# Turning masked scores on TensorE instead of the DMA crossbar for the first two of eight batches

## The chip, the core and the metric

The kernel runs on one core of a Trainium2 chip. The core has a matrix engine (TensorE, PE in the profile; its weight loads are PEld), a vector engine (VectorE, DVE), a scalar engine (ScalarE, ACT), GpSimd (POOL), a queue engine that issues DMAs (SyncE, SP), and 16 DMA engines. TensorE writes to PSUM, in banks; VectorE and ScalarE read PSUM and SBUF; DMAs move data between HBM and SBUF and inside SBUF. The metric is the device time of the core in microseconds, lower is better.

## The reference

Attention with a threshold over 8 batches, 8 heads, 576 positions and 64 dimensions a head, and a layer pair behind it on 4608 tokens, d_model 512 and d_ff 2048:

```python
scores = scale * np.matmul(q, k.transpose(0, 1, 3, 2))
thresh = np.max(scores, axis=-1, keepdims=True) - tau
scores = np.where(scores >= thresh, scores, -1000000000.0)
scores = scores - np.max(scores, axis=-1, keepdims=True)
attn = np.exp(scores)
attn = attn / (np.sum(attn, axis=-1, keepdims=True) + 1e-09)
out = np.matmul(attn, v)
...
h = x @ w_in
g = h - np.tanh(h)
return (g @ w_out).astype(np.float32)
```

Inputs and outputs are float32; x is the attention output with the heads of a token side by side.

## The kernel before, in words

**Pairs and tiles.** Two heads of a batch form a pair p; there are 32 pairs, four to a batch. A pair's queries are cut into nine tiles of 128 rows (TPP = 9): four of one head, one mixed tile with the last 64 rows of both, four of the other head. There are 288 tiles, i = 9p + j. `kind(j)` calls the tiles "A" (j = 0, 2, 5, 7), "B" (1, 3, 6, 8) and "M" (4).

**A tile's way.** `scores` (L215): TensorE multiplies qT with kT and with kS (the same with its two 64-row halves swapped) into psS, a PSUM tile of two banks of which there are two (ps_big, shared with the turns of k and q); VectorE copies it to sc and takes the row's maximum (L242). `shift` (L248): VectorE makes nb, tau minus the maximum. `kink` (L256): ScalarE applies a Prelu with an extreme slope, which leaves kept scores and makes dropped ones hugely negative; the result z is bf16 in SBUF, with an A tile and its B tile side by side in one z of 1152 columns, and the M tile in zm, padded to 640. Then SP issues a crossbar transpose by DMA, zT from z (L274), one for each A-B pair of tiles and one for M, so five a pair. `weights` (L280): ScalarE takes Exp of zT into pT, of 1152 columns for two tiles, 640 for M. `attend` (L290): TensorE multiplies pT with v (psO); `norm` divides by the row sums; `emit_x` (L338) turns the pair's output into psX and xT.

**Feeding a pair.** `load` brings k, q and v by DMA (L130 to L137), `split` (L143) makes of k or q a high and a low fp16 part (GpSimd, but for pair 0 ScalarE and VectorE), `turn` (L176) turns them by nine TensorE transposes, VectorE copies the result to kT or qT (L186), and for all pairs but the first two DMAs make kS from kT (L202, L203). The two layers' weights come in 16 pieces of 512 KB (`w_load`, L460 and L456), one every four steps, cast by GpSimd four steps later (`w_cast`, L448).

**The layers.** `layers(m, tail)` gives the steps for batch m's first layer (`hidden`: four matmuls into psH, L366, then Tanh on ScalarE and g on VectorE) and batch m-1's second (`project` into psY, L392). psY lies in the pool ps_y, one bank, with one buffer. Batch 0's first layer is handed out from pair 4's fifth tile on, one `hidden` in every second step, the first in step 41; psY is first used in the next stage, from step 77 on.

**The order.** Everything is written out by hand in the loop over steps s = -7 to 292. In step s come shift(s+6), scores(s+7), kink(s+5), the tanh of the last layer step, weights(s), layer steps, attend(s-2), and the planned steps of the next pairs: k's load stands 16 steps before the pair's first scores, its split 8, k's turn 5, v's split 4, q's turn 3. Each engine runs its queue in this order, and SP issues all DMAs but pair 0's load of q, which ScalarE's queue issues.

```python
    for t in ("k", "q", "v"):
        load(0, t)
    for t in ("k", "q"):
        split(0, t, fast=True)
        turn(0, t)
```

Of the kernel before, what the change touches and what calls it, by code (L numbers as in the profile page):

```python
# [9 lines left out]
F32 = mybir.dt.float32  # L10
BF16 = mybir.dt.bfloat16
FP16 = mybir.dt.float16
AX = mybir.AxisListType
ALU = mybir.AluOpType
ACT = mybir.ActivationFunctionType
# [3 lines left out]
def kernel(  # L19
# [11 lines left out]
    nc = tc.nc  # L31
    P = 128

    B, H, S, D = q.shape
# [11 lines left out]
    HPAIR = H // 2  # L46
# [2 lines left out]
    DF_C = d_ff // P  # L49
    TPP = 9  # L50
    NTILE = NPAIR * TPP
    W = 2 * S

    AHEAD = 7
# [9 lines left out]
    const = ctx.enter_context(tc.tile_pool(name="const", bufs=1))  # L64
    ident_f16 = const.tile([P, P], FP16, name="ident_f16")
    make_identity(nc, ident_f16)
    ident_bf = const.tile([P, P], BF16, name="ident_bf")
# [35 lines left out]
    zt_pool = pool("zt", 4)  # L103
    p_pool = pool("p", 3)
# [9 lines left out]
    ps_y = pool("ps_y", 1, space=PSUM)  # L114

    ctx.enter_context(tc.manual_schedule())


    raws = {}
# [23 lines left out]
    def split(p, t, fast=False):  # L143
        r = raws.pop((p, t))[:, 0:9, :]
        hl = hl_pool.tile([P, TPP, 2, D], FP16, name=f"{t}hl", tag=t)
        if fast:
            nc.scalar.mul(out=hl[:, :, 0, :], in_=r, mul=QKSC)
            nc.vector.scalar_tensor_tensor(  # L148
                out=hl[:, :, 1, :], in0=r, scalar=QKSC, in1=hl[:, :, 0, :],
                op0=ALU.mult, op1=ALU.subtract,  # L150
            )
        else:
            x = hl_pool.tile([P, TPP, D], F32, name="xs", tag="xs")
            nc.gpsimd.tensor_scalar(  # L154
                out=x, in0=r, scalar1=QKSC, scalar2=1.0, op0=ALU.mult, op1=ALU.mult
            )
            nc.gpsimd.tensor_copy(out=hl[:, :, 0, :], in_=x)
            nc.gpsimd.tensor_tensor(  # L158
                out=hl[:, :, 1, :], in0=x, in1=hl[:, :, 0, :], op=ALU.subtract
            )  # L160
        hls[p, t] = hl

    def split_v(p):
        r, vb = raws.pop((p, "v")), vbs[p % NV]
        nc.gpsimd.tensor_copy(
            out=vb[:, :, 0:4, 0:D],
            in_=r[:, 0:8, :].rearrange("p (h c) d -> p h c d", h=2),
        )
        nc.gpsimd.tensor_copy(out=vb[0:64, :, 4, 0:D], in_=r[0:64, 8:10, :])
        nc.gpsimd.tensor_copy(out=vb[64:P, :, 5, 0:D], in_=r[64:P, 8:10, :])  # L170
# [5 lines left out]
    def turn(p, t):  # L176
        hl = hls.pop((p, t))
        ps = ps_big.tile([P, W], FP16, name=f"ps_{t}", tag="big")
        for c in range(TPP):
            nc.tensor.matmul(  # L180
                out=ps[:, c * P : (c + 1) * P],
                lhsT=hl[:, c, :, :].rearrange("p a d -> p (a d)"),
                rhs=ident_f16, is_transpose=True, start=True, stop=True,
            )
        m = qk_pool.tile([P, W], FP16, name=f"{t}T", tag=t)
        nc.vector.tensor_copy(out=m, in_=ps)  # L186
        mats[p, t] = m
        if t == "k" and p == 0:
            ps = ps_big.tile([P, W], FP16, name="ps_ks", tag="big")
            for c in range(TPP):  # L190
                for a in range(2):
                    nc.tensor.matmul(
                        out=ps[64 * a : 64 * a + 64, c * P : (c + 1) * P],
                        lhsT=hl[:, c, 1 - a, :],
                        rhs=ident_f16, is_transpose=True, start=True, stop=True,
                    )
            sw = qk_pool.tile([P, W], FP16, name="kS", tag="ks")
            nc.vector.tensor_copy(out=sw, in_=ps)
            mats[p, "ks"] = sw
        elif t == "k":  # L200
            sw = qk_pool.tile([P, W], FP16, name="kS", tag="ks")
            nc.sync.dma_start(out=sw[0:D, :], in_=m[D:P, :])  # L202
            nc.sync.dma_start(out=sw[D:P, :], in_=m[0:D, :])  # L203
            mats[p, "ks"] = sw


    MAIN = (slice(0, 512), slice(640, W))
    REM = (slice(512, 576), slice(576, 640))
    scs, zs, zts, pts, ops = {}, {}, {}, {}, {}

    def kind(j):

        return "M" if j == 4 else "A" if j in (0, 2, 5, 7) else "B"

    def scores(i):  # L215
        p, j = divmod(i, TPP)
        qT, kT, kS = mats[p, "q"], mats[p, "k"], mats[p, "ks"]
        ps = ps_big.tile([P, 1024], F32, name="psS", tag="big")
        main, rem, lo = slice(0, 512), slice(512, 576), 0
        if kind(j) == "B":  # L220
            main, rem, lo = slice(512, 1024), slice(448, 512), 448
        if j == 4:
            for n, kk in enumerate((kT, kS)):
                for dst, srcs in ((main, MAIN), (rem, REM)):
                    for hh in range(2):
                        nc.tensor.matmul(  # L226
                            out=ps[64 * hh : 64 * hh + 64, dst],
                            lhsT=qT[:, REM[hh]], rhs=kk[:, srcs[hh]],
                            start=(n == 0), stop=(n == 1),
                        )  # L230
        else:
            hh = int(j > 4)
            lhs = qT[:, j * P : (j + 1) * P]
            for n, kk in enumerate((kT, kS)):
                for dst, src in ((main, MAIN[hh]), (rem, REM[hh])):
                    nc.tensor.matmul(  # L236
                        out=ps[:, dst], lhsT=lhs, rhs=kk[:, src],
                        start=(n == 0), stop=(n == 1),
                    )
        sc = sc_pool.tile([P, S], F32, name="sc")  # L240
        mx = st_pool.tile([P, 1], F32, name="mx", tag="mx")
        nc.vector.tensor_scalar(  # L242
            out=sc, in0=ps[:, lo : lo + S], scalar1=SC, scalar2=None,
            op0=ALU.mult, op1=ALU.max, accum_out=mx,
        )
        scs[i] = sc, mx

    def shift(i):  # L248
        sc, mx = scs[i]
        nb = st_pool.tile([P, 1], F32, name="nb", tag="nb")  # L250
        nc.vector.tensor_scalar(  # L251
            out=nb, in0=mx, scalar1=-1.0, scalar2=tau, op0=ALU.mult, op1=ALU.add
        )
        scs[i] = sc, nb

    def kink(i):  # L256
        sc, nb = scs.pop(i)
        kd = kind(i % TPP)
        if kd == "B":
            zt = zs.pop(i - 1)  # L260
            z = zt[:, S:W]
        elif kd == "A":
            zt = zs[i] = z_pool.tile([P, W], BF16, name="z")
            z = zt[:, 0:S]
        else:
            zt = zms[i // TPP % NM]
            z = zt[:, 0:S]
        nc.scalar.activation(  # L268
            out=z, in_=sc, func=ACT.Prelu, bias=nb, scale=1.0, alpha=STEEP
        )  # L270
        if kd != "A":
            n = 5 if kd == "M" else TPP
            t = zt_pool.tile([P, TPP, P], BF16, name="zT")
            nc.sync.dma_start_transpose(  # L274
                out=t[:, 0:n, :],
                in_=zt,
            )
            zts[i] = t

    def weights(i):  # L280
        kd = kind(i % TPP)
        if kd != "A":
            n = 5 if kd == "M" else TPP
            pt = p_pool.tile([P, TPP * P], FP16, name="pT")
            nc.scalar.activation(  # L285
                out=pt[:, 0 : n * P], in_=zts.pop(i)[:, 0:n, :], func=ACT.Exp
            )
            pts[i] = pt

    def attend(i):  # L290

# [83 lines left out]
    def bend():  # L375
        while halves:
            m, n, ps = halves.pop(0)
            th = t_pool.tile([P, MB], F32, name="th")
            nc.scalar.activation(out=th, in_=ps, func=ACT.Tanh)  # L379
            ths.append((m, n, ps, th))  # L380
# [101 lines left out]
        load(0, t)  # L482
    for t in ("k", "q"):
        split(0, t, fast=True)
        turn(0, t)
    split_v(0)
    for t in ("k", "q", "v"):
# [6 lines left out]
    for at in sorted(plan):  # L494
        if at < -AHEAD:
            plan.setdefault(-AHEAD, []).extend(plan.pop(at))
    for s in range(-AHEAD, NTILE + LAG + 3):
        p, j = divmod(max(s, 0), TPP)
        if 0 <= s < NTILE and j == 2 + LAG and p % HPAIR == 0 and p >= HPAIR:
            assert not todo  # L500
            todo = layers(stage, False)
            share = len(todo) / (HPAIR * TPP - 2 - LAG)
            done, stage = 0.0, stage + 1
        if 0 <= s + AHEAD - 1 < NTILE:
            shift(s + AHEAD - 1)
        if 0 <= s + AHEAD < NTILE:
            scores(s + AHEAD)
        if 0 <= s + MASK < NTILE:
            kink(s + MASK)
        bend()  # L510
        if 0 <= s < NTILE:
            weights(s)
# [77 lines left out]
```

## Time and profile before

| what | us |
|---|---|
| median of three runs | 606.67 (606.66 to 607.59) |
| the profiled execution, its own time | 608.25 |
| its span | 606.5 |
| TensorE busy | 526.2 |
| VectorE busy | 442.8 |
| ScalarE busy | 439.7 |
| GpSimd busy | 215.8 |

The page gives busy times by engine, and the span in 40 slices in which each digit is a busy share in tenths; PEclk is the granted clock of TensorE in tenths. The view of stages gives the same for chosen stretches, with the DMA engines' share (1.00 is all sixteen with work; queued packets can bring it above that). A row of the timeline has the start, the duration, the engine, the line, the operation, what is written and read, and how many instructions are merged in the row; in brackets stands the idle time before it and what ended it. Instructions that follow one another without a wait overlap a little, so what one costs is read from start to start. The view of waits has who waited for what, the sum, the number of times and the longest.

### The profile page before, as it was taken

The numbers are of one execution on the slowest core, as the hardware profiler recorded it, in microseconds if no ns is written. First come the engines' busy times: TensorE is split into PE (matmuls) and PEld (weight loads), VectorE is DVE, ScalarE is ACT, GpSimd is POOL, SyncE is SP. The second block draws the span as 40 slices with busy tenths as digits, with TensorE's granted clock in tenths as the row PEclk, the third lists the DMA queues.
The fourth block names the chain that finished last, engine by engine and source line by source line (L and its number), as shares of the span: only waits on it lengthen the run. The fifth ranks groups of instructions, "written<-read, shape, count | busy, mean of one in ns | idle before, by whom it ended". The sixth has DMA issues, their size and how long they took to land.

```text
span 606.5 us, 13212 instructions
## 1 busy us (share of the span) xinstructions
PE 526.2 (87%) x4749; PEld 291.4 (48%) x4818; DVE 442.8 (73%) x1311; ACT 439.7 (73%) x601; POOL 215.8 (36%) x310
## 2 busy tenths in 40 slices
PE   2757576887899999999999999999999999999990
PEld 1334343444455555555555555555555555444440
DVE  2657465877988898889878888888888888544410
ACT  1576476877998988998798888989898989433310
POOL 6263365339444444444444444444444400000000
PEclk9888687997999999999999999999999999999996
DMA  4699999999898978999997898899888975111011
GB/s 141 146 207 206 208 223 223 218 215 210 188 180 162 195 178 178 202 199 179 163 186 180 197 186 199 193 174 187 190 192 184 200 146 112 52 47 42 35 41 46
DMA packets 230187, 100.21 MB, mean 165 GB/s; under 512 B 193897, under 2 KB 218473, under 8 KB 230121
## 3 DMA queue, kind: packets, MB, share of 16 engines
q1 hardware_dynamic: 229718, 99.06, 78.6%
q8 instruction: 38, 0.62, 0.5%
q10 hardware_dynamic: 402, 0.29, 0.1%
q14 instruction: 29, 0.23, 0.1%
HBM read 37.75 MB, written 9.44 MB: 78 GB/s over the span
## 4 chain that ended last, share of the span: by engine, by line
PE 67%; DMA 9%; issue 8%; DVE 7%; POOL 4%; ACT 3%; SPq 0%; POOLq 0%; ACTq 0%; DVEq 0%
PE psY L392 18%; PE psH L366 16%; PE psS L236 15%; PE psO L316 5%; PE ps_k L180 3%; DVE sc L242 3%; PE psS L226 2%; PE psHt L366 2%; DMA wt<-in_moe_w_in_dram 2%; PE ps_q L180 2%; DMA kS<-kT 2%; DMA out_dram<-yo 2%; DMA zT<-z 1%; DMA kraw<-in_k_dram 1%; PE psO L304 1%
## 5 line engine op out<-in xcount | busy, mean ns | idle before, releaser
L242 DVE TENSOR_SCALAR_CACHE_REDUCE sc<-psS 128x576 f32<-128x576 f32 x288 | 216.6, 752 | 43.2 <-PE psS L236 28.3
L268 ACT ACTIVATE z<-sc,nb 128x576 bf16<-128x576 f32 x256 | 193.4, 765 | 30.3 <-DVE nb L251 28.9
L285 ACT ACTIVATE pT<-zT 128x1152 f16<-128x1152 bf16 (+1 forms) x160 | 170.7, 1067 | 44.7 <-DMA zT<-z 40.4
L392 PE MATMUL psY<-w_out_sb,g 128*128 128x512 bf16 x538 | 138.4, 379 | 3.1 <-issue 1.7
L236 PE MATMUL psS<-kS,qT 128*128 128x512 f16 (+1 forms) x512 | 111.2, 301 | 20.7 <-DMA kS<-kT 20.7
L236 PEld LDWEIGHTS <-qT 128*128 128x128 f16 x1024 | 77.7, 101 | 102.6 <-issue 25.8
L366 PE MATMUL psH<-xT,w_in_sb 128*128 128x512 bf16 x450 | 119.3, 381 | 2.8 <-DVE g L385 0.8
L236 PE MATMUL psS<-kT,qT 128*128 128x512 f16 (+1 forms) x512 | 110.3, 299 | 12.7 <-DVE nb L251 6.8
L385 DVE SCALAR_TENSOR_TENSOR g<-th,psH 128x512 bf16<-128x512 f32 x128 | 87.5, 684 | 33.5 <-ACT th L379 33.5
L379 ACT ACTIVATE th<-psH 128x512 f32<-128x512 f32 x128 | 74.4, 581 | 20.4 <-PE psH L366 19.9
L154 POOL TENSOR_SCALAR xs<-kraw 128x576 f32<-128x576 f32 x31 | 20.9, 673 | 175.7 <-DMA kraw<-in_k_dram 118.7
L392 PEld LDWEIGHTS <-g 128*128 128x128 bf16 x576 | 49.6, 98 | 57.7 <-issue 2.5
L366 PEld LDWEIGHTS <-w_in_sb 128*128 128x128 bf16 x576 | 48.9, 98 | 58.2 <-issue 5.7
L316 PEld LDWEIGHTS <-pT 128*128 128x128 f16 x1280 | 56.8, 100 | 34.1 <-ACT pT L285 8.7
L316 PE MATMUL psO<-vb,pT 128*128 128x65 bf16 x1280 | 63.3, 197 | 4.6 <-ACT pT L285 4.6
L251 DVE TENSOR_SCALAR nb<-mx 128x1 f32<-128x1 f32 x288 | 42.7, 148 | 3.4
L158 POOL TENSOR_TENSOR qhl<-xs,qhl 128x576 f16<-128x576 f32 x31 | 39.7, 1281 | 2.6
L158 POOL TENSOR_TENSOR khl<-xs,khl 128x576 f16<-128x576 f32 x31 | 39.7, 1280 | 2.6
L268 ACT ACTIVATE zm<-sc,nb 128x576 bf16<-128x576 f32 x32 | 24.7, 773 | 19.2 <-DVE nb L251 19.1
L180 PE MATMUL ps_k<-ident_f,khl 128*128 128x128 f16 x288 | 23.5, 231 | 12.7 <-DVE khl L148 9.1
L186 DVE COPY qT<-ps_q 128x1152 f16<-128x1152 f16 x32 | 24.2, 756 | 11.9 <-PE ps_q L180 11.9
L331 DVE TENSOR_TENSOR osb<-psO,rc 128x320 bf16<-128x320 f32 x64 | 29.3, 458 | 2.2
(53 smaller groups left out, 428.2 us busy)
## 6 DMA issues: line engine op xcount, KB each, us to landing
out_dram<-yo SPq DMA_DIRECT2D x36, 256.0 KB
kS<-kT SPq DMA_DIRECT2D x62, 144.0 KB
kraw<-in_k_dram SPq DMA_DIRECT2D x32, 256.0 KB
vraw<-in_v_dram SPq DMA_DIRECT2D x32, 256.0 KB
qraw<-in_q_dram SPq DMA_DIRECT2D x31, 256.0 KB
wt<-in_moe_w_in_dram SPq DMA_DIRECT2D x8, 512.0 KB
wt<-in_moe_w_out_dram SPq DMA_DIRECT2D x8, 512.0 KB
vraw<-in_v_dram SPq DMA_DIRECT2D x64, 32.0 KB
```

The lines of the kernel that those rows point to most:

```text
L158: nc.gpsimd.tensor_tensor(out=hl[:, :, 1, :], in0=x, in1=hl[:, :, 0, :], op=ALU.subtract)
L180: nc.tensor.matmul(out=ps[:, c * P : (c + 1) * P], lhsT=hl[:, c, :, :].rearrange("p a d -> p (a d)"), rhs=ident_f16, is_transpose=True, st ...
L236: nc.tensor.matmul(out=ps[:, dst], lhsT=lhs, rhs=kk[:, src], start=(n == 0), stop=(n == 1),)
L242: nc.vector.tensor_scalar(out=sc, in0=ps[:, lo : lo + S], scalar1=SC, scalar2=None, op0=ALU.mult, op1=ALU.max, accum_out=mx,)
L251: nc.vector.tensor_scalar(out=nb, in0=mx, scalar1=-1.0, scalar2=tau, op0=ALU.mult, op1=ALU.add)
L268: nc.scalar.activation(out=z, in_=sc, func=ACT.Prelu, bias=nb, scale=1.0, alpha=STEEP)
L285: nc.scalar.activation(out=pt[:, 0 : n * P], in_=zts.pop(i)[:, 0:n, :], func=ACT.Exp)
L316: nc.tensor.matmul(out=po[:, (j - 1 - 5 * hh) + ab, :], lhsT=pt[:, blk * P : (blk + 1) * P], rhs=vb[:, hh, c, :], start=(n == 0), stop=(n ...
L366: nc.tensor.matmul(out=ps, lhsT=w_in_sb[:, c, n * P : (n + 1) * P], rhs=xs[m][:, c, :] if m < B else xR[:, c, :, :], start=(c == 0), stop= ...
L379: nc.scalar.activation(out=th, in_=ps, func=ACT.Tanh)
L385: nc.vector.scalar_tensor_tensor(out=gs[m][:, n, :], in0=th, scalar=-1.0, in1=ps, op0=ALU.mult, op1=ALU.add,)
L392: nc.tensor.matmul(out=ps, lhsT=gs[m][:, n, ms * P : (ms + 1) * P], rhs=w_out_sb[:, n, :], start=(n == 0), stop=(n == DF_C - 1),)
```

## The change

There are three parts. First, for the tiles below NPE = 72 (the eight pairs of batches 0 and 1, steps 0 to 71) no crossbar transpose is issued. Instead `weights` has TensorE turn the tile's z by four or five matmuls with the identity into psZ, a bf16 tile of 640 columns in the pool ps_y (one buffer), and ScalarE takes Exp straight from PSUM into the tile's part of pT. An A tile has its own Exp of 512 columns, B and M tiles have 640; A and B share a pT as before. From tile 72 on everything is as before. Second, a one-element Exp runs first of all on ScalarE, so the activation table is loaded there. Third, pair 0's two splits stand ahead of its two turns.

```diff
+    NPE = 2 * HPAIR * TPP
...
+    warm = const.tile([P, 1], F32, name="warm")
+    nc.vector.memset(warm, 0.0)
+    nc.scalar.activation(out=warm, in_=warm, func=ACT.Exp)
...
-        if kd != "A":
+        if i < NPE:
+            zts[i] = zt
+        elif kd != "A":
             n = 5 if kd == "M" else TPP
-            t = zt_pool.tile([P, TPP, P], BF16, name="zT")
-            nc.sync.dma_start_transpose(
-                out=t[:, 0:n, :],
-                in_=zt,
-            )
-            zts[i] = t
+            zts[i] = zt_pool.tile([P, TPP, P], BF16, name="zT")
+            nc.sync.dma_start_transpose(out=zts[i][:, 0:n, :], in_=zt)
 
     def weights(i):
         kd = kind(i % TPP)
-        if kd != "A":
-            n = 5 if kd == "M" else TPP
+        n, off = {"A": (4, 0), "M": (5, 0), "B": (5, 4)}[kd]
+        if i < NPE:
+            z = zts.pop(i)
+            ps = ps_y.tile([P, 5 * P], BF16, name="psZ", tag="y")
+            for c in range(n):
+                nc.tensor.matmul(
+                    out=ps[:, c * P : (c + 1) * P],
+                    lhsT=z[:, (off + c) * P : (off + c + 1) * P],
+                    rhs=ident_bf, is_transpose=True, start=True, stop=True,
+                )
+            if kd == "B":
+                pt = pts.pop(i - 1)
+            else:
+                pt = p_pool.tile([P, TPP * P], FP16, name="pT")
+            nc.scalar.activation(
+                out=pt[:, off * P : (off + n) * P], in_=ps[:, 0 : n * P], func=ACT.Exp
+            )
+        elif kd == "A":
+            return
+        else:
+            n += off
             pt = p_pool.tile([P, TPP * P], FP16, name="pT")
             nc.scalar.activation(
                 out=pt[:, 0 : n * P], in_=zts.pop(i)[:, 0:n, :], func=ACT.Exp
             )
-            pts[i] = pt
+        pts[i] = pt
...
     for t in ("k", "q"):
         split(0, t, fast=True)
+    for t in ("k", "q"):
         turn(0, t)
```

ScalarE's order in the stage with batch 0's first layer, before, from an M tile's Prelu (zm) on; z is a Prelu, th a tanh, pT an Exp:

```order
L268 ACTIVATE zm_93<-sc,nb 128x576
L379 ACTIVATE th<-psH 128x512
L285 ACTIVATE pT<-zT 128x1152
L268 ACTIVATE z<-sc,nb 128x576 x2
L379 ACTIVATE th<-psH 128x512
L285 ACTIVATE pT<-zT 128x1152
```

The same place in the changed kernel:

```order
L274 ACTIVATE zm_93<-sc,nb 128x576
L404 ACTIVATE th<-psH 128x512
L302 ACTIVATE pT<-psZ 128x640
L274 ACTIVATE z<-sc,nb 128x576
L302 ACTIVATE pT<-psZ 128x512
L274 ACTIVATE z<-sc,nb 128x576
L404 ACTIVATE th<-psH 128x512
```

Where one Exp of 1152 columns followed two Prelus, an Exp of 512 or 640 now follows each, and its source is the bank psZ instead of zT in SBUF.

SP's order of issues in pair 0, before, from the third load of k on (wt is a piece of the layers' weights):

```order
L130 DMA kraw<-in_k_dram 128x2x256
L139 DMA kraw<-in_k_dram 128x1x64
L274 DMA_TRANSPOSE zT<-z 128x9x128
L130 DMA qraw<-in_q_dram 128x2x256
L139 DMA qraw<-in_q_dram 128x1x64
L460 DMA wt<-in_moe_w_in_dram 128x1024
L202 DMA kS<-kT 64x1152
L203 DMA kS<-kT 64x1152
```

The same place in the changed kernel:

```order
L136 DMA kraw<-in_k_dram 128x2x256
L145 DMA kraw<-in_k_dram 128x1x64
L136 DMA qraw<-in_q_dram 128x2x256
L145 DMA qraw<-in_q_dram 128x1x64
L485 DMA wt<-in_moe_w_in_dram 128x1024
L208 DMA kS<-kT 64x1152
L209 DMA kS<-kT 64x1152
```

The transpose that stood ahead of q's next load and of the weights is gone; the rest keeps its order.

## The prediction

> **What bounds the kernel now.** I read the page's slices first, then cut the span into stages with the windows view, then the waits inside the slowest stage. The slices show a kernel with two halves:
>
> ```profile
> PEclk9888687997999999999999999999999999999996
> DMA  4699999999898978999997898899888975111011
> ```
>
> One slice is 15.2 us. In the first ten or eleven the DMA engines are full and the granted TensorE clock dips; after them the clock is flat. To cut at events of the program I take the copies of qT on VectorE (pair p's stands in step 9p-10; here those of pairs 0 and 1, and of 9 and 10) and the first matmuls of psH, in step 41:
>
> ```profile
> L186 DVE COPY qT<-ps_q x2: 754/756/758, 14.1 to 23.3; 128x1152 f16<-128x1152 f16 x2
> L186 DVE COPY qT<-ps_q x2: 758/758/758, 160.4 to 174.1; 128x1152 f16<-128x1152 f16 x2
> 104.90 0.92 PE L366 MATMUL psH<-xT,w_in_sb 128*128 128x512 bf16 x3 [0.22 <-issue]
> ```
>
> The cuts are 23.3 us (step -1), 104.9 (step 41), 160.4 (step 71) and 174.1 (step 80):
>
> ```profile
> 23.30:104.90 81.60, 51.06 (x491) 30.15 (x492) 48.42 (x160) 51.19 (x66) 40.27 (x52) 0.77 1.05 214
> 104.90:160.40 55.50, 45.03 (x463) 26.36 (x470) 44.15 (x134) 45.60 (x63) 28.98 (x41) 0.94 0.99 213
> 174.10:520.00 345.90, 336.42 (x3248) 189.11 (x3299) 298.88 (x899) 299.46 (x410) 130.72 (x187) 1.00 0.89 180
> ```
>
> The columns are the stage, its length, then busy time of PE, PEld, DVE, ACT and POOL, the granted clock, the DMA share and GB/s. I call the first two rows stages A and B. A has 42 steps in 81.6 us, 1.94 us a step, and no compute engine is busy for more than 51.2 us of it. B has 30 steps at 1.85 us. From 174.1 us on PE is busy for 336.4 of 345.9 us: that part is bound by TensorE and does not change. What ends the waits in A:
>
> ```profile
> POOL w_in_sb L448 <- DMA wt<-in_moe_w_in_dram: 40.7, 6, 11.6
> ACT pT L285 <- DMA zT<-z: 24.4, 9, 4.9
> PE psS L236 <- DMA kS<-kT: 17.1, 4, 6.1
> ```
>
> All three are DMA. So A is bound by the DMA queue, and the change takes the crossbar's transposes out of exactly the steps 0 to 71.
>
> **The start.** The table load moves ahead of the data, and both splits ahead of both turns.
>
> ```profile
> 0.74 0.49 ACTq L130 DMA_DIRECT2D qraw<-in_q_dram  x1
> 6.24 1.28 ACT L147 ACT_TABLE_LOAD   x1 [6.24 <-DMA kraw<-in_k_dram]
> 8.13 0.67 ACT L147 ACTIVATE qhl<-qraw 128x576 f16<-128x576 f32 x1
> 8.96 0.06 DVE L82 MEMSET vb<- 64x2 bf16 x1
> 9.72 0.06 DVE L83 MEMSET vb<- 64x2 bf16 x1
> 10.24 0.76 DVE L186 COPY kT<-ps_k 128x1152 f16<-128x1152 f16 x1 [0.47 <-PE ps_k L180]
> 11.35 0.76 DVE L198 COPY kS<-ps_ks 128x1152 f16<-128x1152 f16 x1 [0.35 <-PE ps_ks L192]
> 12.03 0.85 DVE L148 SCALAR_TENSOR_TENSOR qhl<-qraw,qhl 128x576 f16<-128x576 f32 x1
> 12.93 1.14 PE L180 MATMUL ps_q<-ident_f,qhl 128*128 128x128 f16 x9 [1.62 <-DVE qhl L148]
> 14.93 0.66 PE L236 MATMUL psS<-kT,qT 128*128 128x512 f16 x2 [0.85 <-DVE qT L186]
> ```
>
> k's split no longer pays the 1.28 us, and q's second half no longer stands behind the copy of kS at 11.35. But q's load is issued on ScalarE's queue, behind the table load now: 1.28 us and a tiny activation later, so about 1.5 us. No row shows when q landed; I bound it by k's 6.24 and q's use at 8.13, so 7.7 to 9.6 now. Its halves (0.67 and 0.85) are then done by 9.3 to 11.2. Behind them stand on VectorE the eight fills (8.96 to 9.78), the copy of kT (0.76), which frees the buffer for ps_q (1.14), and the copy of qT (0.76): 3.6 us with the signals between, so the first psS comes between 12.9 and 14.8 instead of 14.93. I take 13.6, 1.3 us saved, with bounds of 0 and 2.0.
>
> **Stage A, step by step.** What ScalarE does when nothing holds it, by starts (z is the Prelu, pT the Exp of 640, th a tanh of 512 that reads PSUM):
>
> ```profile
> 118.12 0.76 ACT L268 ACTIVATE z<-sc,nb 128x576 bf16<-128x576 f32 x1
> 118.78 0.72 ACT L285 ACTIVATE pT<-zT 128x640 f16<-128x640 bf16 x1
> 119.41 0.76 ACT L268 ACTIVATE z<-sc,nb 128x576 bf16<-128x576 f32 x1
> 120.08 0.58 ACT L379 ACTIVATE th<-psH 128x512 f32<-128x512 f32 x1
> 120.55 0.77 ACT L268 ACTIVATE z<-sc,nb 128x576 bf16<-128x576 f32 x1
> ```
>
> A Prelu takes 0.66 us, an Exp of 640 0.63, a tanh of 512 from PSUM 0.47. In the changed steps each tile has an Exp of its own, four of 512 and five of 640 in nine steps. No row shows an Exp that reads bf16 from PSUM; the two rows bound it, 0.47 and 0.63, and if it gained nothing and lost the overlap it would be 0.58 and 0.72. With the first, ScalarE needs 0.66 + (4 x 0.47 + 5 x 0.63)/9 = 1.22 us a step, 51.2 us in A: what it is busy now, so splitting the Exps costs next to nothing. TensorE's work, by starts, when its clock is full, and one piece where it is not:
>
> ```profile
> 100.32 0.67 PE L236 MATMUL psS<-kT,qT 128*128 128x512 f16 x2
> 100.80 0.67 PE L236 MATMUL psS<-kS,qT 128*128 128x512 f16 x2
> 107.70 0.41 PE L236 MATMUL psS<-kT,qT 128*128 128x512 f16 x2
> 107.94 0.41 PE L236 MATMUL psS<-kS,qT 128*128 128x512 f16 x2
> 108.19 1.03 PE L366 MATMUL psH<-xT,w_in_sb 128*128 128x512 bf16 x4
> 113.03 0.48 PE L316 MATMUL psO<-vb,pT 128*128 128x65 bf16 x10
> 113.34 0.41 PE L236 MATMUL psS<-kT,qT 128*128 128x512 f16 x2
> 115.45 1.03 PE L366 MATMUL psH<-xT,w_in_sb 128*128 128x512 bf16 x4
> 116.31 0.41 PE L236 MATMUL psS<-kT,qT 128*128 128x512 f16 x2
> 125.37 0.66 PE L180 MATMUL ps_q<-ident_f,qhl 128*128 128x128 f16 x9
> 125.88 0.41 PE L236 MATMUL psS<-kT,qT 128*128 128x512 f16 x2
> ```
>
> A tile's scores take 0.49 us (107.70 to 108.19), psO 0.31, four matmuls of psH 0.86, nine transposes 0.51, so 0.057 each. The change adds 41 transposes in nine steps, 0.26 us a step. With psO in five steps of nine (0.17), two turns (0.11) and psX's six (0.04) TensorE needs 1.07 us a step, less than ScalarE.
>
> The new wait: psZ has one buffer, so the transposes of a tile wait for the Exp of the tile before, and that tile's Exp waits for them. Behind the waiting transposes on TensorE stand psO, turns and the next scores. The round holds because a Prelu stands between two Exps on ScalarE: five transposes and their drain are 0.28 + 0.15 us (nine start the next work after 0.51 but last 0.66), with 0.10 allowed for two signals 0.53, inside the Prelu's 0.66. psO and scores (0.31 + 0.49) run under the Exp and the start of the Prelu. So a plain step costs 1.29 us: 1.22, and 0.07 of lost overlap. A turn (0.51) or psX (0.34) comes on top of a step, less the little slack it has: 0.45, 0.45 and 0.30 in nine steps. That is 1.42; for VectorE, busy 48.4 us in A and sharing the score buffers, I add 0.05. 42 x 1.47 = 61.7 us. Of kS's 17.1 us of waits I keep 3, because its queue still carries weights and loads. Stage A then takes 64.7 us and saves 16.9. Bounds: 42 x 1.29 = 54.2 us, and 78.8 us if all 17.1 stay.
>
> The DMA left must fit. 214 GB/s over 81.6 us are 17.5 MB; the transposes in it, four of 295 KB and one of 164 KB a pair over 42/9 pairs, are 6.3 MB. 11.2 MB are left: 52 us at 214 GB/s, 62 us at the 180 GB/s of the last row. It fits, but barely. SP also loses five issues a pair that each wait for a Prelu ahead of later loads.
>
> **Stage B.** Every second step carries psH, and its tanh. From one transposed tile to the next TensorE then does 0.86 + 0.31 (in five of nine) + 0.49 + 0.28, that is 1.63 or 1.94 us, against ScalarE's 0.63 + 0.66 + 0.47 = 1.76. The mean of the larger is 1.86; with a plain step of 1.29 beside it 1.58. Turns and psX add 0.13, VectorE's extra work (the g) by my choice 0.09: 1.80, so 30 x 1.80 = 54.0 us against 55.5 now, 1.5 saved: what the DMA gives back here, the single bank mostly takes. Bounds: 48.0 us at 1.60 and 66.0 at 2.20. In step 67 the crossbar takes over again, as before; nothing after 160.4 us changes.
>
> **The sum.** 1.3 + 16.9 + 1.5 = 19.7 us. The profiled execution took 608.25 us (its span of 606.5 and 1.75 around it), so 588.5 for it; the median of the runs, 606.67, lies 1.58 lower, which gives 587.0.
>
> **A rule that speaks against it.** The clock in this trace falls after TensorE stands idle, and stays up when it is merely half busy:
>
> ```profile
> 58.20:61.60 3.40, 1.01 (x16) 0.56 (x14) 1.93 (x8) 2.57 (x4) 0.47 (x1) 0.87 0.88 230
> 61.60:65.00 3.40, 2.60 (x22) 1.59 (x22) 1.69 (x5) 0.54 (x1) 0.00 (x0) 0.50 0.75 179
> 112.60:116.00 3.40, 1.96 (x22) 1.04 (x21) 2.89 (x10) 3.40 (x6) 1.93 (x2) 1.00 0.90 215
> ```
>
> After a stretch with 1.01 us of work the clock was 0.50; with 1.96 us in 3.4, scores, psO and psH alone, it was 1.00. In a changed step of 1.47 us scores and psO are 0.66 us, 45% against that row's 58%, and all transposes together 0.41. Transposes thus carry the clock or they don't. [...] No row here shows transposes alone over such a stretch. If they count, the forecast stands; if they don't, 45% must do, and where it does not, rival 3 follows.
>
> **The rivals.**
> 1. *The DMA queue keeps the pace of stage A* (0.20). For it: 11.2 MB in 62 us is no reserve, and weights in 512 KB pieces stand ahead of kS in one queue. Against it: the transposes and their blocked issues are gone. 62 us and half of kS's waits, 8.5, are 70.5: 11.1 saved, with start and B 13.9, so 592.8.
> 2. *The bank's round costs more than reckoned in B* (0.10). TensorE and ScalarE are both near full there and neither may run ahead; at 2.20 us a step B loses 10.5, the sum is 7.7, the time 599.0.
> 3. *The clock stays down: slower* (0.06). At half clock scores take 0.96 us (100.32 and 100.80 are 0.48 apart) and all of TensorE's 1.07 us becomes 2.14 a step, over the 1.94 that A takes now; in B, with 0.43 a step for psH, 2 x 1.50 = 3.00. If half of A and B ran so, A would take 42 x (1.47 + 2.14)/2 = 75.8 and 3 for kS, B 30 x (1.80 + 3.00)/2 = 72.0 us: 2.8 saved, 16.5 lost, 1.3 from the start, 12.4 slower, 619.1. It decides once some three steps in ten run at half clock. Against it: a step that lasts 1.47 us leaves no idle stretch like the one at 58.2, and a slow TensorE is a busy one.
> 4. *No change* (0.02): the start gains nothing and A gains what B loses, near 606.
>
> **How the numbers follow.** The forecast has 0.62 and gives 587.0. Its own bounds (A at 1.33 a step without kS's waits, 55.9, B 48.0, start 2.0, together 35.2 saved) reach 571.5, which I hold unlikely all at once, so the low end is 576. The high end takes in rivals 1 and 2: 602. A measurement can tell about 0.2%, 1.2 us, from no change. Faster: 0.62, 0.20, nearly all of 0.10, so 0.90; same 0.03; slower 0.07.
>
> **What would show it.** First psS near 13.6 us; 61 to 67 us from pair 1's copy of qT to the first psH, against 81.6; then 52 to 57 to pair 9's, against 55.5; from pair 10's copy to the end 432.4 us, as now; a granted clock over 0.9 in A; psZ's transposes waiting for ScalarE, each for less than 0.3 us. Waits for kS over 8 us in A mean rival 1, a stage B over 60 us rival 2, a clock under 0.75 in A rival 3. I am wrong altogether if A stays over 78 us.

## The result, and the profile after

The changed kernel takes 578.2 us (four runs, 577.7 to 578.4) against 607.1 for the kernel before beside it (606.7 to 607.8): a ratio of 0.952, with a 95% interval of 0.951 to 0.954. The forecast was 587.0, with a range of 576 to 602: the sign and the bound hold, and the gain is 28.9 us where 19.7 were reckoned. The profiled execution took 578.05 us, its span is 576.3, 30.2 less than before.

The page's slices, the same two rows that opened the prediction (one slice is now 14.4 us):

```profile
PEclk9999999999999999999999999999999999999996
DMA  6556755448889999779989999998999865110111
```

The clock no longer dips, and the DMA engines have room in the first nine slices; from the tenth on, where the crossbar is back, they are as full as before. The stages, cut at the same events (copies of qT of pairs 1, 9 and 10, first psH), with the columns of the prediction's table:

```profile
20.50:77.70 57.20, 50.55 (x682) 35.48 (x682) 48.04 (x160) 51.28 (x83) 36.04 (x49) 1.00 0.69 201
77.70:129.60 51.90, 50.73 (x612) 33.13 (x610) 43.59 (x135) 47.10 (x79) 30.88 (x42) 1.00 0.46 131
129.60:143.30 13.70, 12.73 (x136) 7.31 (x135) 11.79 (x39) 12.30 (x18) 4.73 (x7) 1.00 0.86 180
143.30:489.00 345.70, 339.09 (x3289) 188.53 (x3288) 299.95 (x898) 297.85 (x410) 130.41 (x187) 1.00 0.91 180
```

Stage A went from 81.6 to 57.2 us, stage B from 55.5 to 51.9, the stretch to pair 10 is 13.7 in both, and from there to the end it is 433.0 against 432.4. Before A lie 20.5 us against 23.3. So 24.4 of the 30.2 us come from A, 3.6 from B, 2.8 from the start and the steps up to A, and 0.6 are lost at the end. In A ScalarE is now busy for 51.28 of 57.2 us, in B TensorE for 50.73 of 51.9: A comes close to ScalarE's bound and B to TensorE's. What is left of waiting in A:

```profile
POOL w_in_sb L473 <- DMA wt<-in_moe_w_in_dram: 15.4, 4, 6.3
ACT pT L302 <- PE psZ L293: 5.9, 14, 1.5
PE psZ L293 <- ACT pT L302: 3.6, 12, 0.4
```

TensorE's wait for kS, 17.1 us before, has shrunk to a single one of 0.5 us, and ScalarE's for zT is gone. In their place stands the round over psZ's one buffer: ScalarE waits 5.9 us for turns, TensorE 3.6 us for Exps. A piece of it in the timeline, TensorE and ScalarE:

```profile
60.20 0.38 PE L293 MATMUL psZ<-ident_bf,z 128*128 128x128 bf16 x4
...
60.70 0.59 ACT L302 ACTIVATE pT<-psZ 128x512 f16<-128x512 bf16 x1
...
61.18 0.78 ACT L274 ACTIVATE z<-sc,nb 128x576 bf16<-128x576 f32 x1
61.35 0.44 PE L293 MATMUL psZ<-ident_bf,z 128*128 128x128 bf16 x5 [0.27 <-ACT pT L302]
...
61.84 0.71 ACT L302 ACTIVATE pT<-psZ 128x640 f16<-128x640 bf16 x1
```

The five turns at 61.35 wait for the Exp that ends at 61.29, and are done at 61.79, under the Prelu that began at 61.18; from the first Exp's end to the turns lie 0.06 us, from their end to the next Exp 0.05, and that Exp starts 1.14 us after the last one. The round is there, and here a Prelu covers it.

### The profile page after: what moved, and what is told of

It reads as the page before. It is cut to its first block, busy times and chain, and to the rows that moved or that the text cites. A ratio compares the mean times of both kernels' runs of the same rounds, so it can differ in the third digit from the quotient of the medians.

```text
span 576.3 us, 13882 instructions
## 1 busy us (share of the span) xinstructions
PE 535.3 (93%) x5146; PEld 303.6 (53%) x5146; DVE 442.6 (77%) x1312; ACT 440.1 (76%) x634; POOL 215.6 (37%) x310
## 4 chain that ended last, share of the span: by engine, by line
PE 75%; DMA 6%; ACT 6%; DVE 6%; POOL 2%; issue 1%; SPq 1%; ACTq 0%; POOLq 0%; DVEq 0%
PE psY L417 20%; PE psH L391 17%; PE psS L242 17%; PE psO L341 5%; PE ps_k L186 3%; PE psS L232 3%; ACT pT L302 3%; DVE sc L248 3%; DMA kS<-kT 2%; PE psHt L391 2%; PE psZ L293 2%; ACT z L274 2%; PE psO L329 2%; PE ps_q L186 2%; DMA out_dram<-yo 2%
## 5 line engine op out<-in xcount | busy, mean ns | idle before, releaser
L248 DVE TENSOR_SCALAR_CACHE_REDUCE sc<-psS 128x576 f32<-128x576 f32 x288 | 216.4, 751 | 24.4 <-PE psS L232 10.8
L274 ACT ACTIVATE z<-sc,nb 128x576 bf16<-128x576 f32 x256 | 195.5, 768 | 27.2 <-DVE nb L257 26.0
L417 PE MATMUL psY<-w_out_sb,g 128*128 128x512 bf16 x576 | 145.4, 379 | 0.0
L310 ACT ACTIVATE pT<-zT 128x1152 f16<-128x1152 bf16 (+1 forms) x120 | 127.9, 1066 | 11.6 <-DMA zT<-z 11.0
L391 PE MATMUL psH<-xT,w_in_sb 128*128 128x512 bf16 x480 | 123.4, 379 | 0.0
L242 PE MATMUL psS<-kT,qT 128*128 128x512 f16 (+1 forms) x512 | 105.7, 288 | 8.4 <-DVE nb L257 4.7
L242 PEld LDWEIGHTS <-qT 128*128 128x128 f16 x1024 | 74.8, 98 | 70.7 <-issue 12.4
L242 PE MATMUL psS<-kS,qT 128*128 128x512 f16 (+1 forms) x512 | 105.8, 289 | 2.7 <-DMA kS<-kT 2.6
L341 PE MATMUL psO<-vb,pT 128*128 128x65 bf16 x1280 | 61.2, 193 | 0.6 <-ACT pT L310 0.6
L302 ACT ACTIVATE pT<-psZ 128x640 f16<-128x640 bf16 (+1 forms) x72 | 47.1, 654 | 10.6 <-PE psZ L293 10.5
L274 ACT ACTIVATE zm<-sc,nb 128x576 bf16<-128x576 f32 x32 | 24.7, 773 | 17.3 <-DVE nb L257 17.1
L192 DVE COPY qT<-ps_q 128x1152 f16<-128x1152 f16 x32 | 24.2, 755 | 11.5 <-PE ps_q L186 11.5
L426 DVE COPY yo<-psY 128x512 f32<-128x512 f32 x30 | 20.7, 689 | 13.7 <-DMA out_dram<-yo 8.0
```

Of the source, the lines that this page charges most:

```text
L242: nc.tensor.matmul(out=ps[:, dst], lhsT=lhs, rhs=kk[:, src], start=(n == 0), stop=(n == 1),)
L248: nc.vector.tensor_scalar(out=sc, in0=ps[:, lo : lo + S], scalar1=SC, scalar2=None, op0=ALU.mult, op1=ALU.max, accum_out=mx,)
L274: nc.scalar.activation(out=z, in_=sc, func=ACT.Prelu, bias=nb, scale=1.0, alpha=STEEP)
L302: nc.scalar.activation(out=pt[:, off * P : (off + n) * P], in_=ps[:, 0 : n * P], func=ACT.Exp)
L310: nc.scalar.activation(out=pt[:, 0 : n * P], in_=zts.pop(i)[:, 0:n, :], func=ACT.Exp)
L341: nc.tensor.matmul(out=po[:, (j - 1 - 5 * hh) + ab, :], lhsT=pt[:, blk * P : (blk + 1) * P], rhs=vb[:, hh, c, :], start=(n == 0), stop=(n ...
```

## The experiments

**The theory** is the prediction's: the crossbar's transposes load the DMA engines in the stage in which the weights come in too, so kS, the weights and zT come late. **The rivals**: ScalarE only waited too long for its own zT; SP, which stood waiting for each Prelu, held the later loads back; TensorE's clock; the start. Each ratio is to the kernel before on the same chip, whose runs scattered more there than at first (602.3 to 609.8); the changed kernel's, run again beside some of these, did not (577.7 to 578.9).

**The transposes issued as before, for nobody.** The changed kernel, with this added behind `zts[i] = zt`:

```diff
+            if kd != "A":
+                n = 5 if kd == "M" else TPP
+                x = zt_pool.tile([P, TPP, P], BF16, name="zT")
+                nc.sync.dma_start_transpose(out=x[:, 0:n, :], in_=zt)
```

> The changed kernel, with the crossbar's transposes of the first two batches issued as before into buffers that nobody reads, beside TensorE's turns. Theory (the transposes' load on the DMA engines and their place in SP's queue held stage A back): copies of kS and the weights come late again, stage A (pair 1's copy of qT to the first psH) goes from 57 back to 72 us or more, the time to 592 to 605. Rival (only the way of one tile was too long: ScalarE waited for its own zT): nobody waits for zT here, so A stays at 57 to 60 us and the time at 578 to 582.

Measured 608.0 us, ratio 1.002 (0.999 to 1.005). Its stage A and two of its waits:

```profile
20.90:104.20 83.30, 57.11 (x681) 39.31 (x681) 48.19 (x160) 52.05 (x83) 41.13 (x53) 0.88 1.07 212
```

```profile
POOL w_in_sb L477 <- DMA wt<-in_moe_w_in_dram: 40.0, 6, 9.5
PE psS L242 <- DMA kS<-kT: 21.1, 5, 7.7
```

The whole gain is gone, though nobody reads zT: A is 83.3 us, the waits for kS and the weights are back at 21.1 and 40.0. The time is 3 us above the range expected. That ends the rival of ScalarE's own wait for zT.

**The same load without SP's wait.** The source is a tile of zeros, ready from the start (a GpSimd fill):

```diff
+                nc.sync.dma_start_transpose(out=x[:, 0:n, :], in_=zc[:, 0 : n * P])
```

> As the run with idle transposes, but their source is a tile of zeros that is ready from the start, so SP never stands waiting for a Prelu; the load on the DMA engines and SP's time for the issue stay. If the load is what costs, this takes as long as the run with idle transposes, within 3 us (592 to 605). If SP's standing in wait ahead of later loads is what costs, it falls back to 578 to 584.

Measured 605.5 us, ratio 0.998 (0.995 to 1.001):

```profile
20.60:103.00 82.40, 57.39 (x681) 39.56 (x681) 48.22 (x160) 51.99 (x83) 38.97 (x51) 0.86 1.06 206
```

A is 82.4 us, though SP hardly waits any more (1.2 us between 20 and 80 us, in three waits, none of them for a Prelu). So the transposes do it without SP's standing in wait. The 2.5 us between this and the run before are not told apart from none, since the intervals overlap. What the run keeps, beside the load on the DMA engines, is the time that SP takes to issue a transpose; more on that below.

**SP's wait without the load.** In the same place a copy of 16 rows of 256 bytes:

```diff
+                nc.sync.dma_start(out=x[0:16, 0, :], in_=zt[0:16, 448:576])
```

> The changed kernel, and in place of each former crossbar transpose SP issues a copy of 16 rows of 256 bytes that waits for the same Prelu. It has SP's wait and an issue, next to no load. If the load costs: 578 to 580. If SP's wait costs: over 585, with kS late.

Measured 579.0 us, ratio 0.954 (0.951 to 0.957):

```profile
20.90:80.00 59.10, 50.56 (x681) 35.40 (x681) 47.86 (x160) 51.31 (x83) 39.33 (x52) 1.00 0.65 184
```

A is 59.1 us, 1.9 more than in the changed kernel, against 25 more with the transposes. SP's standing in wait is worth little.

**TensorE's work without the relief.** The kernel before, with the turns of the first 72 tiles done as well, into psZ that nobody reads (the loop of the change, at the head of `weights`).

> The kernel before, with TensorE's turns of the first 72 tiles done as well, into psZ, which nobody reads. Theory (DMA): A stays at 80 us or more, the time at 604 to 612, although TensorE has as much to do as in the changed kernel. Rival (the granted clock): the added work keeps the clock up, over 0.9 in A against 0.77, and the time falls by 5 us or more.

Measured 611.1 us, ratio 1.008 (1.005 to 1.010):

```profile
22.90:104.90 82.00, 57.44 (x682) 39.99 (x682) 47.99 (x158) 51.08 (x65) 39.59 (x52) 0.88 1.04 211
```

The granted clock rose from 0.77 to 0.88, and A stayed at 82.0 us: a higher clock alone gained nothing. The run stops short of the 0.9 that the rival asked for, so what a full clock would do beside the crossbar is not shown. Stage B, where TensorE has less room, grew to 59.2 us.

**Bytes or crossbar.** The run with zeros, with each transpose replaced by a plain copy of the same bytes within SBUF:

```diff
-                nc.sync.dma_start_transpose(out=x[:, 0:n, :], in_=zc[:, 0 : n * P])
+                nc.sync.dma_start(out=x[:, 0:n, :].rearrange("p c n -> p (c n)"), in_=zc[:, 0 : n * P])
```

> As the run whose crossbar transposes of zeros nobody waits for, but each is a plain copy of the same bytes within SBUF. If the bytes are what fills the DMA engines, A takes 80 us or more again and the time is 602 to 606. If a crossbar transpose holds the engines far longer than its bytes (the traces of before and of the changed kernel give 46 us of engine time for 6.0 MB of transposes, 130 GB/s, against 291 GB/s for the rest), the copies add some 21 us of engine time to 39.5: A 60 to 66 us, the time 580 to 588.

Measured 585.7 us, ratio 0.967 (0.965 to 0.970):

```profile
20.60:87.50 66.90, 54.06 (x682) 37.64 (x683) 48.52 (x160) 51.74 (x83) 37.45 (x49) 0.92 0.84 259
```

A is 66.9 us, 0.9 over the range expected, and far from 82.4. The row of the DMA queue that carries all this (packets, MB, share of 16 engines over the span) in the changed kernel, with copies, and with transposes of zeros:

```profile
q1 hardware_dynamic: 186454, 88.31, 70.2%
```

```profile
q1 hardware_dynamic: 192214, 99.06, 73.3%
```

```profile
q1 hardware_dynamic: 229718, 99.06, 79.5%
```

Times the spans (576.3, 584.9 and 605.9 us) these are 404.6, 428.7 and 481.7 us in which packets were under way on all 16 engines. The same 10.75 MB added 24.1 us as 40 copies, 0.60 each, and 77.1 us as 40 transposes, 1.93 each, in 43,264 packets instead of 5,760. Single profiles scatter here: the changed kernel's bytes took 403.1 us in its second profile and 394.3 in the run that leaves out the new start, so both sums are good to some 10 us. The copies differ from the transposes by 53 us, and that is well beyond the scatter. So it is not the bytes that filled the engines, but the way in which the crossbar's transposes move them, at two and a half to three times the engine time or a little more.

Three things differ between the two runs, and no run takes them apart: the crossbar, the size of the packets, and SP's time for an issue. As to size, 41,984 of the transposes' packets have 256 bytes, while the copies' have 1280 or 2304. In the changed kernel the 2,497 packets of 256 bytes between 20 and 80 us, all of plain transfers, took 18 ns each on the mean. At that price 41,984 of them would take an estimated 47 us of 16 engines, so much of the 77 may come with packets of this size. As to the issue, SP, which issues all these DMAs one after the other, took far longer for a transpose of zeros than for the copy in its place:

```profile
31.85 1.58 SPq L284 DMA_TRANSPOSE zT<-zc  x1
```

```profile
42.19 0.49 SPq L284 DMA_DIRECT2D zT<-zc  x1
```

In A a transpose of zeros took 1.82 us of SP on the mean and a copy 0.63, and all issues together fill 78 of 82.4 us there, against 50 of 66.9 with copies. Some of that may be the engines' backlog, which no row shows by itself: behind transposes an issue of q's load took up to 3.07 us, where the same one takes 0.6 in the run with small copies. With the median of 1.34 that a transpose's issue has in the changed kernel from batch 2 on, and the other issues as short as in the run with small copies, SP would need an estimated 61 us for A. So its issues alone would hardly make 82, but how the 25 us divide between SP and the engines is not shown.

**One batch instead of two.** `NPE = HPAIR * TPP`: the crossbar takes over from tile 36 on.

> TensorE turns only the first batch's 36 tiles, the crossbar the second's. Theory (DMA load while the weights come in): the second batch runs at the old pace from step 31 or so on, some 1.8 us a step against 1.55: 10 us over the changed kernel, 586 to 592. If only the first batch mattered: 578 to 581.

Measured 584.0 us, ratio 0.964 (0.962 to 0.967):

```profile
20.50:78.90 58.40, 49.88 (x655) 34.36 (x655) 47.18 (x157) 50.34 (x79) 35.28 (x48) 0.97 0.74 195
78.90:135.30 56.40, 46.26 (x474) 26.61 (x473) 44.86 (x138) 46.93 (x65) 29.89 (x41) 0.94 1.02 215
```

The cost is less than the 586 to 592 expected: of the 27 to 29 us, the first batch alone gives 22. The 58.4 us in A are 1.2 more than with both batches, the 56.4 in B 4.5 more, with the DMA share back at 1.02.

**The start alone, and the rest without it.** The kernel before with the early table load and both splits ahead of the turns; and the changed kernel without these two edits.

> The kernel before with the early table load and both splits ahead of the turns, nothing else. The first psS comes 2.6 us earlier, as in the changed kernel. If the start adds to the rest: 604.0 to 605.0. If the DMA queue sets the pace of stage A from its own start, the 2.6 us are waited away there and the time stays at 606 to 607.

> The changed kernel with the start of the kernel before. If the parts add up: 2.6 us over the changed kernel, 580.3 to 581.3. If the start alone is worth nothing, 578 to 579.

The start alone: 605.8 us, ratio 0.998 (0.996 to 1.001), which cannot be told from none and lies between the two ranges expected. Its first psS came at 12.70 us instead of 14.93, but its stages were these:

```profile
21.00:101.90 80.90, 50.94 (x491) 30.00 (x491) 47.87 (x157) 50.72 (x65) 39.39 (x52) 0.75 1.07 214
101.90:159.70 57.80, 46.50 (x473) 26.26 (x472) 44.46 (x137) 46.40 (x64) 29.63 (x41) 0.93 1.00 207
```

B is 2.3 us longer than in the profile of before, so by its end the lead is 0.7. With one profile of each this is a hint that a DMA-bound stretch waits a lead away, not a proof. The turns alone: 579.8 us, ratio 0.957 (0.955 to 0.959), and its stages are 57.1 and 51.9. Its time is 1.6 us over the changed kernel's, below the 2.1 to 3.1 expected, on another chip than the changed kernel's runs.

**Two banks for psZ.** In steps before 41 the pool of psH is free, so every second tile can go there:

```diff
-            ps = ps_y.tile([P, 5 * P], BF16, name="psZ", tag="y")
+            pl, tag = (ps_h, "h") if i % 2 and i < 40 else (ps_y, "y")
+            ps = pl.tile([P, 5 * P], BF16, name="psZ", tag=tag)
```

> The changed kernel with psZ of every second tile below 40 in the pool of psH, which is free until step 41. By the prediction's account of the single bank a plain step costs 1.29 us of which 0.07 is the round, and turns come on top of it: A falls from 57.2 by 2 to 4 us, the time to 574 to 576. If ScalarE's own work is the bound and the round is hidden, within 1 us of 578.2.

> The run with two banks once more, to stand beside the changed kernel on the same chip. In its first profile stage A took 55.8 us against 57.2, and B the same 51.9: 1.4 us less than the changed kernel. If the single bank costs nothing that shows, no difference beyond 0.5 us.

> The changed kernel once more, beside the following runs on one chip: 577.5 to 579.

First 576.5 us, ratio 0.952 (0.949 to 0.954). Then, with the changed kernel on the same chip, 576.1 us (575.7 to 577.2) against 578.2 (577.7 to 578.9), ratios 0.952 (0.950 to 0.954) and 0.955 (0.953 to 0.957): no run of one lies among the other's, though the intervals against the kernel before overlap. Its stage A in the second run:

```profile
20.70:76.50 55.80, 49.39 (x682) 35.19 (x683) 47.89 (x162) 50.26 (x83) 36.81 (x49) 0.97 0.70 205
```

55.8 against 57.1 us on that chip: the second bank gains about 1.3 us in A, less than the 2 to 4 expected. ScalarE still waits 5.5 us for turns there, but in 5 waits instead of 14, and 3.1 us of it are one wait for a turn of k, which was 1.5 with one bank. That turn waited 2.3 us for k's split, which stood in GpSimd's queue behind the cast of a weight piece that waited 4.6 us for its DMA. So the 1.3 us are a net, and the bank's own cost may be larger. It is the version with the lowest median here.

**Weights sooner, crossbar sooner.** Two banks, `NPE = 5 * TPP`, and a piece of the weights every three steps (`3 * i + 3`).

> Two banks for psZ below tile 40, the weights' pieces every three steps instead of four, and the crossbar from tile 45 on, when the weights are in. Stage A has DMA to spare (share 0.69), so it should stay at 55 to 58 us; stage B loses TensorE's turns and should run near the 1.52 us a step of pair 9: 46 to 49 us against 51.9. The time 571 to 575. If the crossbar's load alone, without weights, still holds B back: 576 to 582.

Measured 577.1 us (574.6 to 579.7), ratio 0.953 (0.951 to 0.956), not the 571 to 575 expected:

```profile
21.00:80.70 59.70, 51.26 (x682) 36.51 (x683) 47.98 (x160) 50.84 (x83) 39.28 (x51) 0.94 0.73 218
80.70:130.20 49.50, 43.51 (x476) 26.02 (x484) 42.92 (x134) 45.65 (x66) 28.59 (x40) 1.00 0.85 184
```

B fell to 49.5 us, 2.2 to 2.4 less than with TensorE's turns, but A grew by 3.9 over the two-bank run. The waits in A say where to:

```profile
PE ps_k L186 <- POOL khl L164: 6.1, 3, 2.9
```

TensorE waits 6.1 us for k's splits, against 3.1 with the weights every four steps, and ScalarE 8.9 us for turns against 5.5. In each of the two longest cases the split stood in GpSimd's queue behind a cast that waited for its piece of the weights, 9.3 and 3.9 us.

## Why the prediction was right, and where its sizes were off

**The bound**, the DMA queue with the crossbar's transposes in it, is shown. Putting the transposes back for nobody undoes the change (608.0 us, and 605.5 without SP's wait for a Prelu); putting back SP's wait alone does not (579.0), and TensorE's work alone does not bring the gain (611.1). How much of it is the engines' load, as the prediction had it, and how much SP's time for the issues, stays open.

**Stage A is the mis-sized term.** Reckoned were 61.7 us of work and 3 of waits for kS; measured are 57.2, with 0.5 of waits for kS, so the sign "61 to 67 us" missed. ScalarE's own work was reckoned at 51.2 us and is 51.28, so Exp from PSUM costs about what the two rows said: by starts 0.48 us with 512 columns (60.70 to 61.18 above) and 0.59 with 640 (61.84 to 62.43, where the next Prelu starts). Over that I had put 10.5 us; the profile has 5.9. Which part was too much can be read from one Exp to the next:

```profile
24.00 0.60 ACT L302 ACTIVATE pT<-psZ 128x512 f16<-128x512 bf16 x1
...
28.89 0.70 ACT L302 ACTIVATE pT<-psZ 128x640 f16<-128x640 bf16 x1
29.18 0.68 PE L186 MATMUL ps_k<-ident_f,khl 128*128 128x128 f16 x9
...
30.67 0.60 ACT L302 ACTIVATE pT<-psZ 128x512 f16<-128x512 bf16 x1 [0.41 <-PE psZ L293]
...
31.83 0.69 ACT L302 ACTIVATE pT<-psZ 128x640 f16<-128x640 bf16 x1
31.91 0.66 PE L186 MATMUL ps_q<-ident_f,qhl 128*128 128x128 f16 x9
...
33.38 0.60 ACT L302 ACTIVATE pT<-psZ 128x512 f16<-128x512 bf16 x1 [0.20 <-PE psZ L293]
```

From 24.00 to 28.89 lie four plain steps, without a turn of k or q and without psX: 1.22 us each, which is also the mean of all 28 such steps between A's first and last Exp. The step with k's turn takes 1.78 us, that with q's 1.55, and the four with psX 1.58 to 1.60. So these three cost 0.56, 0.33 and 0.37 us over a plain step, 1.26 in nine steps where 0.45, 0.45 and 0.30 were charged: in sum that term was right. The step that failed is what was laid on every step, 0.07 us of overlap lost in the round and 0.05 for VectorE. A plain step of 1.22 us is ScalarE's work alone, and 42 times 0.12 are 5.0 us, a little more than the 4.5 by which the 61.7 were too high.

The longest of ScalarE's waits, 1.53 us, has another source, which the prediction did not have:

```profile
63.52 1.04 POOL L473 CAST w_in_sb<-wt 128x1024 bf16<-128x1024 f32 x1 [4.65 <-DMA wt<-in_moe_w_in_dram]
...
67.34 0.68 PE L186 MATMUL ps_k<-ident_f,khl 128*128 128x128 f16 x9 [1.05 <-POOL khl L164]
...
68.83 0.60 ACT L302 ACTIVATE pT<-psZ 128x512 f16<-128x512 bf16 x1 [1.53 <-PE psZ L293]
```

A cast waited for its weights, k's split stood behind it on GpSimd, and the turn waited for the split.

**The reserve of the DMA engines** was reckoned too small. 11.2 MB at 180 to 214 GB/s would have taken 52 to 62 us; 11.5 MB went through in 57.2 us at a share of 0.69, 291 GB/s of engine time. The rates I used came from stretches that had transposes in them, and those slow the mean (1.93 us of engine time against 0.60 for a copy of the same bytes, above). That fits with kS's waits, which did not stay at 3 us, and with the failure of rival 1 (0.20).

**Stage B**: 54.0 reckoned, 51.9 measured, with TensorE busy for all but 1.2 us of it, so the reckoning was 2.1 us too high; which of its terms was, is not shown. Rival 2 fell with it. **After it** nothing changed, as said: 13.7 us, and 433.0 against 432.4.

**The start** was to give 1.3 us, at most 2.0, and gave 2.6: the first psS came at 12.33 instead of 14.93. The step that failed is that q's load would stand behind the table load on ScalarE's queue:

```profile
0.73 1.28 ACT L122 ACT_TABLE_LOAD   x1 [0.73 <-PEq L597]
...
1.17 0.43 ACTq L136 DMA_DIRECT2D qraw<-in_q_dram  x1
...
7.28 0.68 ACT L153 ACTIVATE qhl<-qraw 128x576 f16<-128x576 f32 x1 [0.77 <-DMA qraw<-in_q_dram]
...
12.33 0.66 PE L242 MATMUL psS<-kT,qT 128*128 128x512 f16 x2 [0.85 <-DVE qT L192]
```

The issue began at 1.17 us, while the table was still being loaded, 0.43 us later than before and not 1.5, and q was there by 7.28, ahead of the bounds of 7.7 and 9.6. What stood behind q was reckoned well: its halves were done at 8.75, and 3.6 us on makes 12.35. What this lead is worth in the whole time is another matter: about 1.6 us beside TensorE's turns, and nothing that could be told from none alone.

**The clock**, rival 3, stayed at 1.00 in A and in B. Whether transposes carry it, which the prediction left open, could be tried: in the run that only adds turns to the kernel before, A has nearly the same length (82.0 us against 81.6) and otherwise the same matmuls, and the granted clock went up from 0.77 to 0.88. The other runs fall in line, with 0.75 in A for the start alone, and 0.88 and 0.86 for the two that have the turns beside idle transposes by the crossbar. Here the transposes counted. Of the other signs, psZ's waits for ScalarE were to stay under 0.3 us each; the longest is 0.4.

## What to carry to other kernels

The transposes shared SP's queue and the 16 DMA engines with the weights and kS, and with zeros they took 1.93 us of the engines on the mean, where copies of the same bytes took 0.60, and in A 1.82 us of SP against 0.63. So price a transfer in engine time and in the time of its issue, not in bytes alone, and look at what else has to pass in the same stage; the same move was worth 24 us in the stage where the weights came in and 3.6 where TensorE was nearly full already. To find out which of a removed step's costs mattered, put them back one at a time without a reader: its load, its issue, its wait, its work on the other engine; the issue was not put back alone here. Look in what is left for queues that join two jobs: on GpSimd a cast that waited 4.65 us for its weight piece held up k's split, and with it ScalarE for 1.53. And a single buffer between two engines that take turns can cost little where one of them has other work of the same length in between; here a second one gained 1.3 us in 57.

## What the runs showed of the hardware that was not expected

- Forty crossbar transposes within SBUF (32 of 295 KB, eight of 164) took 1.93 us of all 16 DMA engines on the mean, plain copies of the same bytes 0.60, in 1082 and 144 packets each.
- SP took 1.34 us on the median to issue a transpose of 295 KB in the changed kernel, and 0.60 for a plain copy of that size or of 164 KB in the run with copies.
- ScalarE's queue began to issue a DMA 0.44 us after the table load ahead of it had begun, which lasted 1.28.
- Transposes on TensorE alone raised the granted clock of a waiting stage from 0.77 to 0.88.
